# Merging the scores of two local head pairs into one six-bank step

## The chip, the cores and the metric

The kernel runs on one core of a Trainium2 chip. Its engines are TensorE (PE, with its weight loads PEld), VectorE (DVE), ScalarE (ACT), GpSimd (POOL) and SyncE (SP). Each works through its own queue in the order written; semaphores make one wait for another. The metric is device time in microseconds. PE writes its results to PSUM, which has eight banks of 128 partitions x 512 fp32 values; a bank may be filled again once the engine that reads it is through.

## The reference

Eight batches of eight heads, 576 positions, head dimension 64. Heads 0 to 3 attend locally (a key at most 31 positions back), heads 4 to 7 in a stride (keys at the same position modulo 32). The attention output, as 4608 tokens x 512, goes through a feed-forward layer with a squared Relu.

```
scores = q @ k.T / sqrt(64)
local:   0 <= i - j < 32            (heads 0..3)
strided: j <= i and i % 32 == j % 32 (heads 4..7)
attn = softmax(where(mask, scores, -1e9)) @ v
x = attn.transpose(0, 2, 1, 3).reshape(4608, 512)
out = relu(x @ w_in) ** 2 @ w_out        # w_in 512 x 2048, w_out 2048 x 512
```

## The kernel before

**The feed-forward layer is the backbone.** Tokens go in nine chunks of 512. `mm1(c, ff)` makes 128 of the 2048 hidden rows of chunk c with four matmuls of 128 x 512 (L663; one for each of the four tiles `xt[0..3]`, in the order 0, 1, 2, 3), a Relu on ACT into `r` (L669, four buffers) and a square on DVE into `g` (L670). `mm2(c, i)` adds four of the sixteen hidden blocks to 128 output rows (L685); after the fourth part ACT copies the sum to `y` (L689) and SP stores it. Each call is one *group*. Chunk c has groups 32c to 32c+15 (`mm1`) and 32c+16 to 32c+31 (`mm2`). From group 32 on all of them take turns on the two banks called `ph`.

**The attention is woven in by a written plan.** `PLAN` is a list of lines `group: words`. Before a group is issued, the words of its line are run, and each word is a step that issues its instructions on the engines at once; the group comes behind them. After each group `tick()` issues the work that was put off with `later(n, ...)`, n ticks ahead, by due time. So the plan fixes the order in every queue. Batch 0 has a list of its own ahead of group 0. A unit is a pair of heads: unit 4b and 4b+1 are the local pairs of batch b, and 4b+2 and 4b+3 the strided ones.

The words that matter here:

- `S u`: scores of a local pair (L494). One head sits on partitions 0 to 63 and the other on 64 to 127, so matmuls come in pairs that contract over 64 rows each. Six blocks of 96 queries x 128 keys for each head, 12 matmuls in four `pt` banks of 288 columns; then four exps (L504) into the tile `es[u % 4]` and two multiplications by the mask on DVE (L510). With `!` all four exps are issued at once; without, they are spread over the ticks.
- `D u.part`: output of one head of a local pair (L623, six matmuls with 128 columns of `e` as weights, so the last reads 32 columns past the head), then a reciprocal and a multiplication on DVE (L628, L629) into `x`. Before it starts it issues what is still put off for u.
- `E u`: transposes `x` into `xt[0]` or `xt[1]`: by DMA from SP for batches from 2 on (L638), by PE and a copy for batch 1.
- `s b.part` and `x b.part`: scores and products of the strided heads, in three parts. `x` uses two `pt` banks: the sums of weights (L550; Ln and Exp on ACT, L555 and L556, make their inverse) and the products (L553); DVE multiplies them into `xt[2]` and `xt[3]` (L563, L569). `x b.2` writes 64 rows of `xt[3]` for all 576 tokens of batch b.
- `T`, `W`, `k`, `B`, `c`: transposes by PE, copies and casts. `X`, `Y`: DMA transposes on SP. `Q`, `C`, `U`, `V`, `l`, `r`, `o`: loads on POOL. `m..v`: memsets of two block tiles of batch 2 on DVE (L813).

PSUM has five `pt` banks that `bank("pt")` hands out in turn, two `ph` and one `py`. In chunk 0 an `mm2` sum holds one of the `pt` banks, so four are left in turn from group 19 to 31. `py` isn't used after group 31.

Of the kernel before, what the change touches and what calls it, by code (L numbers as in the profile page):

```python
# [9 lines left out]
BF16 = mybir.dt.bfloat16  # L10
AF = mybir.ActivationFunctionType
ALU = mybir.AluOpType
# [8 lines left out]
"""  # L21
PLAN = """
0: l1q4+5 l1k4+5 z
1: r1q U1 mv1g
3: o0 mk0v
4: r1k V1
5: o1 l2k8+9 mbg mv0v
6: o2 o3 V2
8: c4qv
9: c5qv  # L30
# [4 lines left out]
14: S4  # L35
15: W1q1v
16: B10v W1k0a
17: S5! W1k1a
18: k10v mrg C2q C2k
19: k11v D4.0  # L40
20: s1.0 D4.1 B11v
21: s1.1 D5.0 U2
22: l3k12+13 s1.2
23: D5.1 x1.0
24: E4a
25: x1.1
26: E5a X2k l3q12+13
27: x1.2
28: V3
29: c9kv  # L50
# [5 lines left out]
38: T8qv C3k  # L56
39: k20v
40: U3
41: S8! k21v
42: T9qa  # L60
44: S9! D8.0
46: D8.1
47: E8
48: D9.0 Q16k s2.0
49: s2.1
50: Q17q Q16q s2.2 c12kv
51: D9.1 c12qa
52: Q17k c13kv c13qa
54: x2.0 X3q
55: E9 X3k C4k C4q  # L70
56: x2.1
57: T12ka
58: V4 T13qv T12qa
59: T13ka
60: x2.2 B30v
61: B31v
63: U4 S12!
64: X4q
65: D12.0
66: Y17 k30v  # L80
67: Y16 D12.1 S13! X4k C5q k31v
68: C5k
71: s3.0 E12 Q20k Q21q Q20q
72: Q21k s3.1
73: D13.0 D13.1
# [4 lines left out]
83: x3.1  # L90
89: x3.2
90: k40v
91: S16! k41v
95: U5 D16.0 D16.1
96: S17
97: Y20
99: X5k
100: C6k
101: X5q
102: Q25q V5 E16  # L100
# [9 lines left out]
114: k51v  # L110
116: x4.0
119: x4.1
124: V6
125: x4.2
128: U6 S20!
130: S21
133: D20.0
134: Y24 D20.1 X6k
135: E20 X6q s5.0 C7q Q28k
# [8 lines left out]
150: x5.1 k60v  # L128
152: k61v
153: x5.2  # L130
155: S24!
156: V7
157: U7
161: S25
162: D24.0
165: s6.0 D24.1
166: s6.1
# [9 lines left out]
186: x6.2  # L147
188: k70v
189: k71v
191: S28!  # L150
192: S29
197: s7.0
198: D28.0 s7.1
199: D29.0
# [10 lines left out]
def kernel(  # L165
# [9 lines left out]
    nc = tc.nc  # L175
    B, H, S, D = q.shape
# [4 lines left out]
    scale = 1.0 / (D ** 0.5)  # L181
    QL = 96
    NL = S // QL
# [12 lines left out]
    singles = ctx.enter_context(tc.tile_pool(name="singles", bufs=1))  # L196
# [13 lines left out]
    banks = {nm: [psum.tile([128, 512], FP32, name=f"{nm}{i}") for i in range(n)]  # L210
             for nm, n in (("ph", 2), ("py", 1), ("pt", 5))}
# [4 lines left out]
    def bank(nm):  # L216
        if in_b0[0] and nm == "pt":
            nm = "b0"
        t = banks[nm].pop(0)
        banks[nm].append(t)  # L220
        while id(t) in unread:
            run_due(lambda x: x[1] == unread[id(t)])
        return t
# [8 lines left out]
    mask_all = singles.tile([128, NL, QL], BF16)  # L232
# [7 lines left out]
    mask_bd = singles.tile([128, 1, W3], BF16)  # L240
    str_rows_t = {nm: singles.tile([SR, RW], BF16, name=f"{nm}_t") for nm in "qk"}
    kTl = [singles.tile([128, 32 + S], BF16, name=f"kTl{i}") for i in range(NV)]
    es = [singles.tile([128, 1280], BF16, name=f"e{i}") for i in range(4)]
    xt = [singles.tile([128, T], BF16, name=f"xt{p}") for p in range(4)]
    w_in_b = singles.tile([128, 4, d_ff], BF16)
    w_out_b = singles.tile([128, 16, d_model], BF16)
# [14 lines left out]
    st = {}  # L261
# [173 lines left out]
    def later(n, fn, key=None):  # L435
        pending.append((clock[0] + n, key, fn))

    def run_due(test):
        due = [x for x in pending if test(x)]
        for x in due:  # L440
            pending.remove(x)
        for x in sorted(due, key=lambda x: x[0]):
            x[2]()
# [23 lines left out]
    def step_S(u, mode=0):  # L467
# [39 lines left out]
        def masks(row):  # L507
            x = e[0:kn, S * row:S * (row + 1)].rearrange("p (t c) -> p t c", c=w)
            m = mask_all if local else mask_str.to_broadcast([kn, n, w])
            nc.vector.tensor_tensor(x, x, m, op=ALU.mult)  # L510
# [15 lines left out]
        later(3, lambda: expo(1, 1), u)  # L526
        later(4, lambda: masks(1), u)

    def blocks(part):
        return range(NJ * part, min(NJ * (part + 1), NB))  # L530

# [81 lines left out]
                rv.rearrange("c (j p) -> c p j", p=SP_), op=ALU.mult)  # L613

    def step_D(u, part):
        run_due(lambda x: x[1] == u)
        s = st[u]
        e = s["e"]
        rhs = s["v"].rearrange("p h t d -> p (h t) d")
        po = bank("pt")[:, 0:NL * (D + 1)].rearrange("p (n d) -> p n d", d=D + 1)  # L620
        for n in range(NL):
            c = QL * (NL * part + n)
            nc.tensor.matmul(po[:, n, :], e[:, c:c + 128], rhs[:, NL * part + n, 0:D + 1], start=True, stop=True)  # L623
        if part == 0:
            s["x"] = xl_pool.tile([QL, 2 * NL, D], BF16, name="x_l")
        x = s["x"].rearrange("p (t h) d -> p h t d", h=2)[:, part]
        rinv = small.tile([128, NL, 1], FP32, name="rinv")
        nc.vector.reciprocal(rinv[0:QL], po[0:QL, :, D:D + 1])  # L628
        nc.vector.tensor_tensor(x, po[0:QL, :, 0:D], rinv[0:QL].to_broadcast([QL, NL, D]), op=ALU.mult)  # L629
# [66 lines left out]
    A, V, G = nc.scalar.copy, nc.vector.tensor_copy, nc.gpsimd.tensor_copy  # L696
# [32 lines left out]
    def run_step(word):  # L729
        op, arg = word[0], word[1:]  # L730
        if op == "w":
            warm(int(arg))
        elif op == "c":
            cast_qk_local(int(arg[:-2]), arg[-2], ENG[arg[-1]])
        elif op == "T":
            step_T(int(arg[:-2]), arg[-2], ENG[arg[-1]])
        elif op == "W":
            step_TS(int(arg[0]), arg[1], int(arg[2]), ENG[arg[3]])
        elif op == "S":
            step_S(int(arg.rstrip("!")), int("!" in arg))  # L740
        elif op == "N":
            step_N(int(arg))
        elif op == "O":
            step_O(int(arg))
        elif op in "sx":
            (step_SS if op == "s" else step_XX)(*(int(x) for x in arg.split(".")))
        elif op == "k":
            step_K(int(arg[0]), int(arg[1]), ENG[arg[2]])
        elif op == "m":
            memset_later(arg[:-1], nc.gpsimd if arg[-1] == "g" else nc.vector)  # L750
        elif op == "D":
            u, part = arg.split(".")
            step_D(int(u), int(part))
        elif op == "E":
            step_E(int(arg.rstrip("av")), ENG.get(arg[-1]))
        elif op == "P":
            first_part([int(x) for x in arg])
        elif op == "H":
            shift_v_local(int(arg[:-1]), ENG[arg[-1]])
        elif op == "C":  # L760
            load_str_tall(int(arg[:-1]), arg[-1])
        elif op == "Q":
            load_qk_rows(int(arg[:-1]), arg[-1])
        elif op == "X":
            transpose_str(int(arg[:-1]), arg[-1])
        elif op == "Y":
            transpose_local(int(arg))
        elif op == "V":
            load_v_local_all(int(arg))
        elif op == "U":  # L770
            load_v_str(int(arg))
        elif op == "B":
            spread_v_str(int(arg[0]), int(arg[1]), ENG[arg[2]])
        elif op == "l":
            load_qk_local_sw(int(arg[0]), [int(x) for x in arg[2:].split("+")], arg[1])
        elif op == "r":
            load_str_rows(int(arg[0]), arg[1])
        elif op == "i":
            load_w_in(int(arg))
        elif op == "o":  # L780
            load_w_out(int(arg))
        elif op == "z":
            late_constants()
        else:
            raise ValueError(word)
# [100 lines left out]
    for line in PLAN.strip().splitlines():  # L886
        n, words = line.split(":")
        plan.setdefault(int(n), []).extend(words.split())
    for n, g in enumerate(groups):
        for word in plan.get(n, ()):  # L890
            run_step(word)
        g()
        tick()
# [32 lines left out]
```

## Time and profile before

| | us |
|---|---|
| median of 3 runs (303.82 to 304.15) | 303.82 |
| the profiled execution | 303.86 |
| its span | 302.2 |
| PE busy in it | 295.2 (98%) |
| DVE busy | 178.8 (59%) |
| ACT busy | 174.5 (58%) |
| POOL busy | 72.3 (24%) |
| granted TensorE clock | 1.00 |

The span runs from the first to the last instruction; 1.7 us lie around it. Groups of instructions go by their line in the kernel: L663 and L685 are the feed-forward matmuls (131.8 and 121.1 us of PE's busy time), L494 the local scores, L504 their exps, L510 their masks, L550 and L553 the strided products. An arrow in brackets behind a row names what ended the idle time before it. Matmuls are pipelined: one of 512 columns is shown 379 ns long though the next starts earlier, so their rate is read from starts.

### The profile page before, as it was taken

The page shows a single profiled execution, that of the slowest core. Times are in us where ns is not written, and L with a number is a line of the kernel's source. Part 1 is how long each engine was busy: PE and PEld are TensorE (multiplying, and loading weights), DVE is VectorE, ACT ScalarE, POOL GpSimd, SP SyncE. Part 2 cuts the span into 40 slices and gives each one's busy share as a digit, 9 for nine tenths or more (in the row PEclk, how much of TensorE's full clock was granted, in tenths as well). Part 3 has the DMA queues.
Part 4 walks back from the last instruction along what each step waited for, and adds up shares of the span by engine and source line. Part 5 has one row for each costly group of instructions (what it writes and reads, how often), then busy time and mean ns, then how long its engine had stood idle before and what let it go on. Part 6 is the DMA issues. An engine that isn't in the chain of part 4 may idle for free.

```text
span 302.2 us, 5752 instructions
## 1 busy us (share of the span) xinstructions
PE 295.2 (98%) x2181; PEld 146.2 (48%) x2181; DVE 178.8 (59%) x463; ACT 174.5 (58%) x344; POOL 72.3 (24%) x105
## 2 busy tenths in 40 slices
PE   8989999999999999999999999999999999999996
PEld 3543555445545544444445445444454444444444
DVE  5668688688578686585568485666486524104400
ACT  3677855777667743874387447744875346226611
POOL 8835734008104027082300840000000000000000
PEclk9999999999999999999999999999999999999999
DMA  8999999997999999999999999611110110010011
GB/s 157 181 208 200 191 199 193 166 196 117 145 171 159 159 175 190 151 138 123 177 143 151 118 198 177 123 48 68 45 23 20 73 69 0 35 72 35 0 71 70
DMA packets 93643, 37.28 MB, mean 123 GB/s; under 512 B 78956, under 2 KB 87750, under 8 KB 93616
## 3 DMA queue, kind: packets, MB, share of 16 engines
q0 software_dynamic: 54960, 18.82, 62.4%
q1 hardware_dynamic: 38512, 18.03, 31.9%
q8 instruction: 17, 0.28, 0.4%
q14 instruction: 10, 0.08, 0.1%
q10 hardware_dynamic: 144, 0.07, 0.1%
HBM read 38.21 MB, written 9.44 MB: 158 GB/s over the span
## 4 chain that ended last, share of the span: by engine, by line
PE 89%; DVE 4%; POOL 3%; ACT 2%; issue 1%; DVEq 0%; ACTq 0%; POOLq 0%
PE ph L663 39%; PE ph L685 36%; PE pt L494 2%; PE pt L623 2%; DVE xt L563 2%; PE pt L454 1%; PE pt L539 1%; PE pt L553 1%; PE ph L710 1%; PE py L685 1%; PE pt L550 1%; POOL w_in_b L426 1%; DVE g_sb L670 1%; PE pt L685 1%; ACT r L669 1%
## 5 line engine op out<-in xcount | busy, mean ns | idle before, releaser
L663 PE MATMUL ph<-xt,w_in_b 128*128 128x512 bf16 x568 | 131.8, 379 | 0.8 <-ACT xt L648 0.8
L685 PE MATMUL ph<-w_out_b,g_sb 128*128 128x512 bf16 x528 | 121.1, 379 | 0.1
L669 ACT ACTIVATE r<-ph 128x512 bf16<-128x512 f32 x142 | 84.7, 599 | 34.9 <-PE ph L663 30.0
L670 DVE TENSOR_TENSOR g_sb<-r 128x512 bf16<-128x512 bf16 x144 | 60.2, 423 | 65.6 <-ACT r L669 64.9
L663 PEld LDWEIGHTS <-w_in_b 128*128 128x128 bf16 x576 | 53.0, 97 | 59.3 <-issue 1.9
L685 PEld LDWEIGHTS <-g_sb 128*128 128x128 bf16 x560 | 51.7, 97 | 57.2 <-DVE g_sb L670 0.5
L689 ACT COPY y<-ph 128x512 f32<-128x512 f32 x33 | 19.5, 590 | 53.5 <-PE ph L685 53.5
L563 DVE TENSOR_TENSOR xt<-pt,rv 64x144 bf16<-64x144 f32 x84 | 34.0, 405 | 18.0 <-ACT rv L556 16.8
L504 ACT ACTIVATE e<-pt 128x288 bf16<-128x288 f32 (+1 forms) x68 | 24.0, 414 | 7.8 <-PE pt L494 7.7
L629 DVE TENSOR_TENSOR x_l<-pt,rinv 96x384 bf16<-96x384 f32 x30 | 16.6, 554 | 1.0
L555 ACT ACTIVATE rv<-pt 128x432 f32<-128x432 f32 (+1 forms) x21 | 10.5, 501 | 11.1 <-PE pt L550 11.1
L569 DVE TENSOR_TENSOR xt<-pt,rv 64x270 bf16<-64x270 f32 (+1 forms) x28 | 10.9, 432 | 8.5 <-ACT rv L556 8.3
L510 DVE TENSOR_TENSOR e<-e,mask_all 128x576 bf16<-128x576 bf16 x28 | 12.4, 453 | 4.1 <-ACT e L504 3.8
L540 ACT ACTIVATE e<-pt 128x432 bf16<-128x432 f32 (+1 forms) x21 | 10.4, 497 | 6.0 <-PE pt L539 6.0
L351 POOL DMA_DIRECT2D q_t<-in_q_dram x6 | 3.5, 579 | 43.4 <-DMA qT_s<-q_t 43.4
L420 POOL DMA_DIRECT2D vl<-in_v_dram x7 | 10.0, 1435 | 12.7 <-DMA vl<-in_v_dram 10.5
L280 POOL DMA_DIRECT2D k_l<-in_k_dram x16 | 12.1, 761 | 2.8 <-DMA v_st<-in_v_dram 1.7
L280 POOL DMA_DIRECT2D q_l<-in_q_dram x16 | 11.6, 730 | 3.5 <-DMA k_l<-in_k_dram 1.9
L623 PEld LDWEIGHTS <-e 128*128 128x128 bf16 x192 | 9.0, 97 | 5.3 <-issue 0.4
L556 ACT ACTIVATE rv<-rv 128x432 f32<-128x432 f32 (+1 forms) x21 | 11.2, 532 | 0.7
L623 PE MATMUL pt<-vl,e 128*128 128x65 bf16 x180 | 9.9, 193 | 0.0
L351 POOL DMA_DIRECT2D k_t<-in_k_dram x6 | 3.2, 540 | 27.0 <-DMA kT_s<-k_t 27.0
(129 smaller groups left out, 219.7 us busy)
## 6 DMA issues: line engine op xcount, KB each, us to landing
out_dram<-y SPq DMA_DIRECT2D x35, 256.0 KB, 3.7
vl<-in_v_dram POOLq DMA_DIRECT2D x7, 384.0 KB, 12.5
w_in_b<-in_moe_w_in_dram POOLq DMA_DIRECT2D x4, 512.0 KB, 12.3
w_out_b<-in_moe_w_out_dram POOLq DMA_DIRECT2D x4, 512.0 KB, 13.5
q_t<-in_q_dram POOLq DMA_DIRECT2D x7, 288.0 KB, 6.2
k_t<-in_k_dram POOLq DMA_DIRECT2D x7, 288.0 KB, 5.6
v_st<-in_v_dram POOLq DMA_DIRECT2D x7, 216.0 KB, 8.0
k_l<-in_k_dram POOLq DMA_DIRECT2D x16, 72.0 KB, 7.5
```

The lines of the kernel that those rows point to most:

```text
L280: nc.gpsimd.dma_start(out=t[:, :, hh, :], in_=src[b, 2 * p + hh].rearrange("(t p) d -> p t d", p=QL))
L504: nc.scalar.activation(e[0:kn, lo:lo + S // 2], pss[row][half][0:kn, 0:S // 2], AF.Exp, scale=scale)
L510: nc.vector.tensor_tensor(x, x, m, op=ALU.mult)
L556: nc.scalar.activation(rv, rv, AF.Exp, scale=-1.0)
L563: nc.vector.tensor_tensor(to[:, :, NJ * part:NJ * (part + 1), par], of, by, op=ALU.mult)
L623: nc.tensor.matmul(po[:, n, :], e[:, c:c + 128], rhs[:, NL * part + n, 0:D + 1], start=True, stop=True)
L629: nc.vector.tensor_tensor(x, po[0:QL, :, 0:D], rinv[0:QL].to_broadcast([QL, NL, D]), op=ALU.mult)
L663: nc.tensor.matmul(ph, w_in_b[:, kk, 128 * ff:128 * (ff + 1)], xt[kk][:, 512 * c:512 * (c + 1)], start=(kk == order[0]), stop=(kk == order ...
L669: nc.scalar.activation(r, ph, AF.Relu)
L670: later(1, lambda: nc.vector.tensor_tensor(g[:, ff, :], r, r, op=ALU.mult))
L685: nc.tensor.matmul(py, g[:, ff, 128 * j:128 * (j + 1)], w_out_b[:, ff, :], start=(ff == 0), stop=(ff == 15))
L689: nc.scalar.copy(y, py)
```

## The change

Three things change.

- A new word `G b` replaces the two `S` words of batch b, for b from 2 to 7. It computes the scores of both local pairs in one go: 24 matmuls into six `pt` banks of 384 columns (three for each row half), then six exps of 384 columns, issued at once, first those of row half 0; the masks of half 0 come two ticks later and those of half 1 three. The results of both pairs lie in one tile `es01` of 2560 columns, of which `es[0]` and `es[1]` are now slices. `D` reads from the new place for units above 7.
- From group 32 on `py` joins the `pt` banks, which makes six.
- The plan moves words. `G` stands before groups 47, 63, 94, 124, 158 and 191. In batch 2 the steps `D8`, `D9`, `E8`, `E9`, `s2` and `x2` move; `D12`, `D16` and `x4.2` move as well. In batch 1 `S5` moves behind `W1k1a`, and `E5a` ahead of `x1.1`; two DVE memsets move to group 1.

The diff, with plan lines that only lose or shift words around these left out where "..." stands:

```diff
-1: r1q U1 mv1g
-3: o0 mk0v
+1: r1q U1 mv1g mk0v mv0v
+3: o0
 4: r1k V1
-5: o1 l2k8+9 mbg mv0v
+5: o1 l2k8+9 mbg
...
-17: S5! W1k1a
-18: k10v mrg C2q C2k
+17: W1k1a
+18: S5! k10v mrg C2q C2k
...
-25: x1.1
-26: E5a X2k l3q12+13
+25: E5a x1.1
+26: X2k l3q12+13
...
-41: S8! k21v
+41: k21v
 42: T9qa
-44: S9! D8.0
-46: D8.1
-47: E8
-48: D9.0 Q16k s2.0
-49: s2.1
-50: Q17q Q16q s2.2 c12kv
-51: D9.1 c12qa
-52: Q17k c13kv c13qa
-54: x2.0 X3q
-55: E9 X3k C4k C4q
-56: x2.1
-57: T12ka
+47: G2
+48: Q16k
+50: Q17q Q16q c12kv s2.0
+51: c12qa D8.0 s2.1
+52: Q17k c13kv c13qa D8.1
+53: D9.0 E8 s2.2
+54: X3q D9.1
+55: X3k C4k C4q x2.0
+56: E9
+57: T12ka x2.1
...
-63: U4 S12!
+63: G3 U4
 64: X4q
-65: D12.0
 66: Y17 k30v
-67: Y16 D12.1 S13! X4k C5q k31v
-68: C5k
+67: Y16 X4k C5q k31v D12.0
+68: C5k D12.1
...
-91: S16! k41v
-95: U5 D16.0 D16.1
-96: S17
+91: k41v
+94: G4
+95: U5
 97: Y20
-99: X5k
+98: D16.0
+99: X5k D16.1
...
-124: V6
-125: x4.2
-128: U6 S20!
-130: S21
+124: G5 V6
+128: U6 x4.2
...
-155: S24!
...
-161: S25
+158: G6
...
-191: S28!
-192: S29
+191: G7
...
-    es = [singles.tile([128, 1280], BF16, name=f"e{i}") for i in range(4)]
+    es01 = singles.tile([128, 2560], BF16, name="e01")
+    es = [es01[:, 0:1280], es01[:, 1280:2560]] + [singles.tile([128, 1280], BF16, name=f"e{i}") for i in (2, 3)]
...
+    def step_G(b):
+
+        us = (4 * b, 4 * b + 1)
+        bk = [bank("pt") for _ in range(6)]
+        bk = [bk[0::2], bk[1::2]]
+        for t in range(2 * NL):
+            for row in range(2):
+                s, j = st[us[t // NL]], t % NL
+                rows, c = slice(64 * row, 64 * row + 64), QL * (t % 4)
+                nc.tensor.matmul(bk[row][t // 4][:, c:c + QL], s["kT"][rows, QL * j:QL * j + 128],
+                                 s["qT"][rows, QL * j:QL * (j + 1)], start=True, stop=True)
+        e = es01[:, 0:4 * S].rearrange("p (r c) -> p r c", r=2)
+
+        def masks(row):
+            x = e[:, row].rearrange("p (u t c) -> p u t c", u=2, c=QL)
+            for i in range(2):
+                nc.vector.tensor_tensor(x[:, i], x[:, i], mask_all, op=ALU.mult)
+
+        for row in range(2):
+            for i in range(3):
+                nc.scalar.activation(e[:, row, 4 * QL * i:4 * QL * (i + 1)], bk[row][i][:, 0:4 * QL], AF.Exp, scale=scale)
+            later(row + 2, lambda row=row: masks(row), ("G", b, row))
...
-        run_due(lambda x: x[1] == u)
+        run_due(lambda x: x[1] in (u, ("G", u // 4, part)))
         s = st[u]
-        e = s["e"]
+        e = es01[:, 2 * S * part + S * (u % 4):] if u > 7 else es[u % 4][:, S * part:]
...
-            c = QL * (NL * part + n)
+            c = QL * n
...
+        elif op == "G":
+            step_G(int(arg))
...
+        if n == 32:
+            banks["pt"] += banks.pop("py")
```

## The prediction

> **What bounds the kernel now.** I read the page first, then the waits, then the timeline of single engines around the places that the change touches.
>
> ```profile
> span 302.2 us, 5752 instructions
> ...
> PE 295.2 (98%) x2181; PEld 146.2 (48%) x2181; DVE 178.8 (59%) x463; ACT 174.5 (58%) x344; POOL 72.3 (24%) x105
> ```
>
> TensorE (PE) is busy for 98% of the span, so the end is set by its queue: time comes from matmul time taken away, and goes to whatever makes PE wait. ACT and DVE have 40% free on average, but both take their work strictly in the order written, so one burst can hold PE up. Who waits:
>
> ```profile
> ACT r L669 <- DVE g_sb L670: 3.0, 6, 0.7
> ...
> PE pt L494 <- ACT e L504: 0.5, 1, 0.5
> ...
> PE pt L645 <- DVE xt L563: 0.3, 1, 0.3
> ```
>
> The first line says that a Relu cannot start before VectorE has squared an older `r` (four buffers); the other two are batch 1's second scores waiting for an exp, and a transpose waiting for a bank that the strided multiplies still read. Now a score step in mid-run (S12 before group 63), PE alone, then ACT alone; columns are start, length, what:
>
> ```profile
> 85.22 2.75 PE L685 MATMUL ph<-w_out_b,g_sb 128*128 128x512 bf16 x12
> 87.90 0.43 PE L494 MATMUL pt<-qT,kTl 64*128 64x96 bf16 x12
> 88.26 1.04 PE L685 MATMUL ph<-w_out_b,g_sb 128*128 128x512 bf16 x4
> 89.14 1.03 PE L663 MATMUL ph<-xt,w_in_b 128*128 128x512 bf16 x4
> 90.00 0.35 PE L623 MATMUL pt<-vl,e 128*128 128x65 bf16 x6
> 90.19 1.89 PE L663 MATMUL ph<-xt,w_in_b 128*128 128x512 bf16 x8
> ```
>
> ```profile
> 85.12 0.59 ACT L689 COPY y<-ph 128x512 f32<-128x512 f32 x1 [0.23 <-PE ph L685]
> 85.60 0.45 ACT L555 ACTIVATE rv<-pt 128x324 f32<-128x324 f32 x1
> 86.08 0.47 ACT L556 ACTIVATE rv<-rv 128x324 f32<-128x324 f32 x1
> 88.24 1.32 ACT L504 ACTIVATE e<-pt 128x288 bf16<-128x288 f32 x4 [1.69 <-PE pt L494]
> 89.42 0.62 ACT L689 COPY y<-ph 128x512 f32<-128x512 f32 x1
> ```
>
> A big matmul comes every (2.75 - 0.38)/11 = 0.216 us, a group of four takes 0.864. From 85.22 to 88.26 are 3.04 us; twelve big matmuls are 2.59, so the twelve score matmuls cost 0.45. They run as six pairs (two 64-row halves); the last pair starts at 88.33 - 0.20 = 88.13, so a pair takes (88.13 - 87.90)/5 = 0.045, six of them 0.27, and going in and out of these 64-row matmuls about 0.19.
>
> The copy of y (group 63) had its last matmul near 88.92 + 0.38 and started at 89.42, just behind four exps. Group 65 takes the bank that it reads: copy done at 90.04, group 65 at 90.19. The slack is 0.15, with D12.0 (0.18) in between.
>
> **The change part by part.** The sum is against the profiled execution: 303.86 us with a span of 302.2; the median of the runs is 303.82.
>
> *Scores merged, six batches.* G has 24 score matmuls as before, but goes in and out once: 0.19 + 12 x 0.045 against 2 x 0.45, a saving of 0.2 a batch, **-1.2**. Waits that went with the old steps: eight big matmuls take 1.73 us when undisturbed; after S8 they took 1.82 and after S13 1.91 (chain and PE timeline), because Relus stood behind exps: 0.10 + 0.17, **-0.28**.
>
> *ACT under G.* Four exps of 288 columns start (1.32 - 0.42)/3 = 0.30 apart, and the copy followed 1.18 after the first: 0.295 each. For 384 columns I scale to 0.393; six are 2.36, against 8 x 0.295 = 2.36 for two S. ACT's work is unchanged, but it comes in one block. [...]
>
> Let T0 be where PE would have begun the next big matmul. S12 began at T0 + 0.09 and its first exp three pairs and 0.34 later; G's first banks need four pairs: first exp at T0 + 0.47, ACT free at T0 + 2.83.
>
> *G3 before 63 and G7 before 191.* The group runs from T0 + 0.71; its y copy is behind six exps: T0 + 2.83 to 3.43, PE sees it 0.06 later at 3.49. The second group after wants that bank at 0.71 + 2 x 0.864 = 2.44. **+1.05** for G7. D12.0, which hid this before, has moved to 67. Bounds 0.9 (0.37 an exp) to 1.1.
>
> At 63 something else lands too. SP issues transposes in order; before, E9 (x of unit 9) stood ahead of X3k, at 79.80, and X3k at 82.34 held the queue for 3.52. E9 now comes behind X3k and a y store, and E8, moved from 47 to 53, directly ahead of X3q. The issue-to-landing times in that stretch are 8.7 (E9), 10.6 (X3q), 7.4 (X3k), so E9 landed at 88.5, 0.9 before group 64 reads it (89.14 + 0.216). Behind X3k it lands about 1.5 to 2.5 later in the same frame; a miss of 0.6 to 2. It overlaps with the bank's wait, so I take the larger of the two, **+1.3** (1.0 to 2.2).
>
> *G4 (94), G6 (158).* The y copy of 95 or 159 is ready at T0 + 2.64, starts at 2.83, is done by 3.49; group 97 or 161 wants the bank at 3.30. Something under 0.2 each; Relus have slack behind. **+0.15** (0 to 0.4).
>
> *G2 before 47.* Group 46's Relu comes first, so exps begin at T0 + 0.69 and group 47's Relu at 3.05, done at 3.65. On DVE its square (0.34 to the next) stands ahead of the masks, which then run from 4.03 to 4.87 (0.46 each, 0.38 apart). PE reaches D8.0 at 0.71 + 4 x 0.864 + 0.20 (s2.0) = 4.37; its last matmul, 0.15 later, reads into the second mask's columns and sees them at 4.93. **+0.4** (0 to 0.6).
>
> *G5 (124) and x4.2, moved from 125 to 128.* This is the largest term. PE and what follows, before:
>
> ```profile
> 147.84 0.30 PE L550 MATMUL pt<-e,ones_bd 128*128 128x324 bf16 x1
> 147.98 0.32 PE L553 MATMUL pt<-e,vb 128*128 128x54 bf16 x6
> 148.14 2.75 PE L685 MATMUL ph<-w_out_b,g_sb 128*128 128x512 bf16 x12
> 150.82 0.43 PE L494 MATMUL pt<-qT,kTl 64*128 64x96 bf16 x12
> 151.18 1.04 PE L663 MATMUL ph<-xt,w_in_b 128*128 128x512 bf16 x4
> ```
>
> x4.2 at 147.84 makes Ln (148.18), Exp (148.65) and four multiplies into `xt[3]` (149.15 to 150.72): 2.88 us. Chunk 4 (groups 128 to 143) covers tokens 2048 to 2559, and batch 4 begins at 2304, so the fourth matmul of group 128 reads what x4.2 writes. Before, three groups and a score step covered this. Now x4.2 stands directly ahead of 128: position P, products until P + 0.30, fourth matmul wanted at P + 0.95. The copy of y of group 127 is ahead of the Ln on ACT (ready at P + 0.2, the Ln 0.48 after it, as at 85.12 and 85.60), which delays it by 0.34. Multiplies done at P + 2.88 + 0.34 = 3.22, seen at 3.28: **+2.34** (2.0 without the copy, 2.5). PE is in order, nothing passes.
>
> *Front: two memsets to group 1.* They ran at 25.59 (before group 3) and 27.67 (before 5), 1.23 each; now both precede the square of group 3, which goes from 26.74 to about 28.0 to 28.2. The Relu of group 7 waits for it (r buffers), so it starts at 28.4 to 28.7 instead of 27.20, and group 9, which needs its bank, at 29.0 to 29.3 instead of 27.85. Against that T4qa no longer waits for its cast (0.68 before, PE held until 30.25) nor T4kv (0.12). Net 0.35 to 0.67; memsets came after idles of 0.24 and 0.34, so I take **+0.6**; without those idles it is the lower end.
>
> *Batch 1's second scores, 17 to 18.* Group 16 began at 37.03 and group 17 at 39.27: 2.24, of which group 16 is 0.86, S5 0.45 and eight transposes 0.26. The other 0.66 is S5, whose last matmuls waited until 38.77 for the exp of 38.27; with W1k1a ahead, and a group later, the bank is free in time. But E5a and x1.1 share group 25, and its product bank is x1.0's (four banks rotate while a y holds one): x1.0's six multiplies start 46.65 in the new frame and end 49.16, x1.1 wants the bank at 47.94. +1.28, against E5a's old wait of 0.45. -0.66 - 0.45 + 1.28 = **+0.2** (-0.2 to 0.4).
>
> Other moves (x2.0 and x2.1 a group later, D8 and D9 to 51 to 54, U6 and V6 on POOL's queue) issue the same work; I cost them at nothing, since POOL waits 43 us for X transposes anyway and x2.2's bank is now T12ka's, which is read early.
>
> Sum: -1.2 - 0.28 + 1.05 + 1.3 + 0.15 + 0.4 + 2.34 + 0.6 + 0.2 = +4.56, so **308.4**.
>
> **The rivals.**
>
> *x4.2 hidden.* Should the dependence be looser than I read, or P later because ACT and DVE are early, the 2.34 go and 306.1 stays. For it: only 64 rows of `xt[3]` are written. Against: the program must be right, and the columns overlap. 0.1.
>
> *Transposes worse.* The hardware queue ran at landing times of 7 to 11 us there. If E8 and E9 land 3 to 5 late, 310.3 to 312. Against: software loads pause from 79.8 to 90.3 on POOL, and landing later in the run is 3.6. 0.1.
>
> *The other side: the order written is not the order run.* If the queues were filled in another order (copies ahead of exps, x4.2's products ahead of group 125, memsets behind squares), the added waits, 5.84 in all, go and -1.48 + 0.2 remains, 302.6; it decides once no more than 1.3 of the 5.84 is left. Against: at 88.24 the four exps ran in one piece ahead of the copy, and PE's rows follow the plan word by word. 0.07.
>
> **How the numbers follow.** My forecast as summed has 0.72 (306.4 with all low ends, 310.3 with all high), x4.2 hidden 0.1 (305.2 to 306.6), transposes 0.1, the other side 0.07, and 0.01 is unnamed. The range 305.4 to 310.3 leaves out the other side and most of the transposes. About 0.2%, 0.6 us, can be told from no change: faster 0.04, same 0.03, slower 0.93.
>
> **What would show it.** A wait of PE at a L663 matmul on DVE's `xt` of about 2.3 near group 128 and one on ACT's y of about 1 after G7; an ACT group of six 128x384 exps near 2.4; PE on DMA or ACT at group 64; an ACT wait on `g_sb` of over 1 near 28; scores at 0.73 for 24 matmuls. If group 128 starts without that wait, the prediction falls by its largest term.

## The result and the profile after

The changed kernel takes 308.63 us in the median of four executions (308.06 to 309.89), the kernel before beside it 303.82: a ratio of 1.0153, 95% interval [1.0129, 1.0176], so it is slower by 1.5%. The profiled execution is the one of 308.06, with a span of 306.4 against 302.2. The forecast was 308.4 and slower. (Where a kernel below had executions more than 1.5% above its fastest, as the first mended try did, its median and ratio leave these out.)

From the page of the changed kernel, first the span, then TensorE's share, the clock that TensorE was granted in forty slices, and the group of the merged exps (busy us, mean ns | idle before them):

```profile
span 306.4 us, 5689 instructions
...
PE 291.1 (95%) x2144; PEld 146.2 (48%) x2181; DVE 178.8 (58%) x463; ACT 174.1 (57%) x332; POOL 71.3 (23%) x105
...
PEclk9999999999999999999999999999999999999999
...
L544 ACT ACTIVATE e<-pt 128x384 bf16<-128x384 f32 x30 | 12.8, 510 | 6.8 <-PE pt L533 6.8
```

TensorE went from 98% busy to 95%; the other engines do what they did. (Part of PE's fall is only that the trace lacks 37 matmul records: 2144 are listed, 2181 weight loads. A later trace of the same kernel that has them all shows 96%, and there 1.7 us of it are matmuls at half clock.) What PE waits for, in us in total, times, longest:

```profile
PE ph L681 <- DVE xt L587: 2.2, 1, 2.2
PE ph L681 <- ACT y L707: 1.6, 2, 0.8
PE ph L681 <- ACT r L687: 1.4, 1, 1.4
...
PE pt L571 <- DVE xt L581: 1.1, 1, 1.1
```

None of these four lines has a counterpart before. They are, in order: the fourth matmul of group 128 waiting for x4.2's multiplies; groups 65 and 193 waiting for a copy of y; group 9 waiting for a Relu; x1.1 waiting for its bank. Together 6.3 us of new waits, against a span only 4.2 us longer.

The largest one, PE alone, then ACT, then DVE (start, length):

```profile
152.61 0.30 PE L568 MATMUL pt<-e,ones_bd 128*128 128x324 bf16 x1
152.75 0.32 PE L571 MATMUL pt<-e,vb 128*128 128x54 bf16 x6
152.91 0.81 PE L681 MATMUL ph<-xt,w_in_b 128*128 128x512 bf16 x3
155.88 1.45 PE L681 MATMUL ph<-xt,w_in_b 128*128 128x512 bf16 x6 [2.16 <-DVE xt L587]
```

```profile
152.81 0.59 ACT L707 COPY y<-ph 128x512 f32<-128x512 f32 x1 [1.28 <-PE ph L703]
153.29 0.45 ACT L573 ACTIVATE rv<-pt 128x324 f32<-128x324 f32 x1
153.77 0.47 ACT L574 ACTIVATE rv<-rv 128x324 f32<-128x324 f32 x1
```

```profile
154.27 1.55 DVE L587 TENSOR_TENSOR xt<-pt,rv 64x270 bf16<-64x270 f32 x4 [2.25 <-ACT rv L574]
```

Three matmuls of group 128 run, the fourth starts at 155.88, when the four multiplies (end 155.82) are through. Undisturbed it would have come at 152.91 + 3 x 0.216 = 153.56: 2.32 lost. The y copy stands ahead of the Ln, as the forecast had it.

The block of exps and its victim, at G7, PE and then ACT:

```profile
217.00 1.03 PE L681 MATMUL ph<-xt,w_in_b 128*128 128x512 bf16 x4
218.82 1.02 PE L681 MATMUL ph<-xt,w_in_b 128*128 128x512 bf16 x4 [0.80 <-ACT y L707]
```

```profile
215.89 0.87 ACT L544 ACTIVATE e<-pt 128x384 bf16<-128x384 f32 x2 [2.28 <-PE pt L533]
216.65 0.50 ACT L544 ACTIVATE e<-py 128x384 bf16<-128x384 f32 x1
217.02 1.27 ACT L544 ACTIVATE e<-pt 128x384 bf16<-128x384 f32 x3
218.13 0.64 ACT L707 COPY y<-ph 128x512 f32<-128x512 f32 x1
```

Six exps from 215.89 to 218.13, then the copy to 218.77, then group 193 at 218.82. Undisturbed it would have started at 217.00 + 0.864, so 0.96 are lost. Group 65 after G3 loses the same 0.96.

And the front, DVE and ACT:

```profile
26.96 1.23 DVE L833 MEMSET vb<- 128x1408 f32 x1 [0.24 <-issue]
28.11 1.02 DVE L688 TENSOR_TENSOR g_sb<-r 128x512 bf16<-128x512 bf16 x3
```

```profile
28.56 1.09 ACT L687 ACTIVATE r<-ph 128x512 bf16<-128x512 f32 x2 [1.82 <-DVE g_sb L688]
```

The squares start at 28.11, behind both memsets; the Relu of group 7 stands still for 1.82 until the first is done, and group 9 comes at 29.21, 1.54 late. A little later S4 stands longer, too (PE):

```profile
34.91 0.75 PE L489 MATMUL pt<-qT,kTl 64*128 64x96 bf16 x12
```

Before, the same twelve took 0.48. The eighth comes at 35.38, behind VectorE's copy of W1q0v's transposes out of PSUM (34.88 to 35.33), whose bank it needs; before, that copy ended at 34.50 and the eighth came at 34.55.

### The profile page after: what moved, and what is told of

Its sections match the earlier page's. It is cut to its first block, busy times and chain, and to the rows that moved or that the text cites. A ratio compares the mean times of both kernels' runs of the same rounds, so it can differ in the third digit from the quotient of the medians.

```text
span 306.4 us, 5689 instructions
## 1 busy us (share of the span) xinstructions
PE 291.1 (95%) x2144; PEld 146.2 (48%) x2181; DVE 178.8 (58%) x463; ACT 174.1 (57%) x332; POOL 71.3 (23%) x105
## 4 chain that ended last, share of the span: by engine, by line
PE 86%; ACT 5%; DVE 4%; issue 2%; DMA 2%; POOL 0%; DVEq 0%; ACTq 0%; POOLq 0%
PE ph L681 37%; PE ph L703 35%; DMA w_out_b<-in_k_dram 2%; DVE xt L581 2%; PE pt L641 1%; ACT e L544 1%; PE pt L557 1%; PE ph L728 1%; PE py L703 1%; PE pt L571 1%; PE pt L533 1%; PE pt L568 1%; ACT r L687 1%; PE pt L703 1%; PE pt L449 1%
## 5 line engine op out<-in xcount | busy, mean ns | idle before, releaser
L703 PE MATMUL ph<-w_out_b,g_sb 128*128 128x512 bf16 x511 | 118.4, 379 | 1.3 <-issue 0.6
L581 DVE TENSOR_TENSOR xt<-pt,rv 64x144 bf16<-64x144 f32 x72 | 29.1, 404 | 14.9 <-ACT rv L574 14.0
L544 ACT ACTIVATE e<-pt 128x384 bf16<-128x384 f32 x30 | 12.8, 510 | 6.8 <-PE pt L533 6.8
L540 DVE TENSOR_TENSOR e<-e,mask_all 128x576 bf16<-128x576 bf16 x24 | 9.9, 456 | 8.7 <-ACT e L544 8.7
L573 ACT ACTIVATE rv<-pt 128x432 f32<-128x432 f32 (+1 forms) x18 | 9.0, 502 | 9.9 <-PE pt L568 9.9
L647 DVE TENSOR_TENSOR x_l<-pt,rinv 96x384 bf16<-96x384 f32 x24 | 13.3, 553 | 0.8
L587 DVE TENSOR_TENSOR xt<-pt,rv 64x270 bf16<-64x270 f32 (+1 forms) x24 | 9.3, 429 | 7.0 <-ACT rv L574 6.9
L571 PEld LDWEIGHTS <-vb 128*128 128x128 bf16 x154 | 7.1, 97 | 4.8 <-issue 1.3
```

What stands on the lines that cost most here:

```text
L544: nc.scalar.activation(e[:, row, 4 * QL * i:4 * QL * (i + 1)], bk[row][i][:, 0:4 * QL], AF.Exp, scale=scale)
L571: nc.tensor.matmul(po[:, c], vb[:, t, :], e[:, c], start=True, stop=True)
L581: nc.vector.tensor_tensor(to[:, :, NJ * part:NJ * (part + 1), par], of, by, op=ALU.mult)
L703: nc.tensor.matmul(py, g[:, ff, 128 * j:128 * (j + 1)], w_out_b[:, ff, :], start=(ff == 0), stop=(ff == 15))
```

## The experiments

Twelve kernels ran. Each was compared with the kernel before on the same chip; its ratio comes from that. For the size of single terms I also give the lowest time, to be set against the changed kernel's lowest, 308.06. The runs come from three chips; the kernel before has nearly the same lowest time on each of them (303.75, 303.66, 303.67). The waits given as "extra" are read from the starts of the big matmuls: spacing, less 0.216 for each, less the small matmuls between them.

### x4.2 ahead of group 121

```
 119: x4.1
+121: x4.2
 124: G5 V6
-128: U6 x4.2
+128: U6
```

> The changed kernel with x4.2 before group 121 and nothing else moved. My theory (group 128 reads what x4.2 writes into xt[3], and three groups used to cover its 2.9 us): the wait of 2.3 us at group 128's fourth matmul goes, the profiled span falls from 306.4 to about 304.1, the median from 308.6 to about 306.3. Rival (the wait is one for a bank that G5 holds, or for the DMA of E17, and x4.2 was only the last to be seen): the wait stays at group 128 or appears at x4.2 or G5, at least 1.8 us of it, and the time moves by less than 0.5.

Measured 306.15 (305.93 to 307.93), ratio 1.0064 [1.0043, 1.0084], span 304.2. Group 128 runs through without a gap. From lowest to lowest it is -2.13, against the 2.32 of the wait. The rest is a new wait of 0.22 in the scores of G5: x4.2's four multiplies now run from 147.76 to 149.32, and G5's last seven matmuls start at 149.38. The largest term of the forecast stands, and its rival (the dependence looser than read) falls. About half of the loss against before comes from the place of one word in the plan.

### x4.2 one group earlier

```
+127: x4.2
-128: U6 x4.2
+128: U6
```

> x4.2 is issued one group earlier, at 127 in place of 128. Theory that the wait at group 128 is the fixed chain of 3.2 us behind x4.2: one group of 0.86 covers part of it, wait at the fourth matmul 2.33 - 0.86 = 1.47 us (1.1 to 1.5, since the copy of y of group 127 now comes behind the Ln), 307.2 us at clock 1.0. On the clock: the front's wait of 1.54 us never went with a fall of the granted clock, the one of 2.2 to 2.3 did in half of the executions. If the length of the pause decides, no execution has clock .994 (all near 307.2); if any pause of over 1 us at this place does it, about half are near 308.8 with clock .994.

Measured 306.96 (306.83 to 307.05), ratio 1.0103 [1.0089, 1.0117]. ACT, and then PE:

```profile
152.77 0.47 ACT L575 ACTIVATE rv<-rv 128x324 f32<-128x324 f32 x1
153.32 0.59 ACT L708 COPY y<-ph 128x512 f32<-128x512 f32 x1
```

```profile
154.89 1.46 PE L682 MATMUL ph<-xt,w_in_b 128*128 128x512 bf16 x6 [0.96 <-DVE xt L588]
```

The extra is 1.12, at the low end: one group covers 0.86, and the copy of y now comes behind the Ln and the Exp, which frees the other 0.34 that the forecast had put on it (2.33 - 0.86 - 0.34 = 1.13). So the chain behind x4.2 is the forecast's, link by link. All four executions had the full clock, which the section on the clock below needs.

### The two memsets back to groups 3 and 5

```
-1: r1q U1 mv1g mk0v mv0v
-3: o0
+1: r1q U1 mv1g
+3: o0 mk0v
-5: o1 l2k8+9 mbg
+5: o1 l2k8+9 mbg mv0v
```

> The changed kernel with the two DVE memsets again before groups 3 and 5. My theory (the pair in one piece delays the square of group 3, so the Relu of group 7 has no r buffer and group 9 no bank): the wait of 1.5 us at group 9 goes, but the one of 0.7 at the first transpose of batch 1's q and 0.1 at the next come back; net -0.66 us. Rival (PE waits there for what arrives by DMA, whatever the memsets do): the waits at group 9 keep over 1 us, net within 0.2.

Measured 307.5 (307.06 to 308.92), ratio 1.0109 [1.0081, 1.0137]. Group 9's wait is gone, S4 takes what it took before, and the old waits at T4qa (0.61) and T4kv (0.30) are back: -1.54 - 0.27 + 0.61 + 0.30 = -0.9. Lowest to lowest -1.0.

### A fifth buffer for the Relus

```
-    r_pool = ctx.enter_context(tc.tile_pool(name="r_pool", bufs=4))
+    r_pool = ctx.enter_context(tc.tile_pool(name="r_pool", bufs=5))
```

> The changed kernel with five r buffers in place of four, memsets where the change put them. My theory (the Relu of group 7 waits for the square of group 3 behind the memsets): now it is group 8's Relu that waits for that square, so PE stops at group 10 and not at 9, about 0.6 in place of 1.5, and up to 0.3 of it shows at the first transpose behind its cast; net -0.6 to -0.9 us. Rival (PE waits for the loads or for the casts behind the memsets): the whole 1.5 us stays, in that place or at the transpose.

Measured 308.89 (307.6 to 309.26), ratio 1.0127 [1.0088, 1.0166]. The wait moves on by one group, to group 10, and shrinks from 1.54 to 0.67; T4qa and T4kv wait again for 0.14 and 0.11, S4 by 0.24 less than in the changed kernel. Net -0.86 in the trace, within the -0.6 to -0.9 expected; lowest to lowest it is only -0.46, from three executions at full clock, so the time shows less than the trace. The move and the shrinking of the wait are what the theory asks for: it was the buffers of `r` through which the memsets reached TensorE.

### The last three exps spread over the ticks

```
-        for row in range(2):
-            for i in range(3):
-                nc.scalar.activation(...)
-            later(row + 2, lambda row=row: masks(row), ("G", b, row))
+        def expo(row, i):
+            nc.scalar.activation(...)
+        for i in range(3):
+            expo(0, i)
+            later(i + 1, lambda i=i: expo(1, i), ("G", b, 1))
+        later(2, lambda: masks(0), ("G", b, 0))
+        later(4, lambda: masks(1), ("G", b, 1))
```

> The changed kernel with the last three exps of each G put off by one, two and three ticks, so that copies and Relus come between. My theory (the six exps in one block keep the copy of y, and so a ph bank): the waits of 0.96 at groups 65 and 193, of 0.1 at 97 and 161 and of 0.3 at D8.0 go, together -2.4 us. Rival 1 (group 64 or 65 has to wait for the transposed x of E9 anyway): -1.5, with a wait on a DMA at 64. Rival 2 (a Relu that shares its group with an exp takes over 0.86 us, so Relus fall behind one after another): of the 2.4 some 1 to 2 come back as waits of 0.1 to 0.3 at the groups behind G3 and G7.

Measured 307.79 (306.17 to 308.93), ratio 1.0112 [1.0083, 1.0141]; lowest to lowest -1.89. PE and ACT at G7:

```profile
216.02 3.19 PE L685 MATMUL ph<-xt,w_in_b 128*128 128x512 bf16 x14
```

```profile
215.66 0.50 ACT L543 ACTIVATE e<-py 128x384 bf16<-128x384 f32 x1
216.22 0.59 ACT L711 COPY y<-ph 128x512 f32<-128x512 f32 x1
216.70 0.50 ACT L543 ACTIVATE e<-pt 128x384 bf16<-128x384 f32 x1
217.08 0.60 ACT L691 ACTIVATE r<-ph 128x512 bf16<-128x512 f32 x1
```

The copy of y slips in behind the third exp and group 192 runs on into 193 without a gap. The waits at 65, 97, 161, 193 and D8.0 are all gone (0.96 + 0.10 + 0.10 + 0.96 + 0.32 = 2.44); a new one of 0.46 stands at D12.1, whose mask now comes last, so the trace gives -1.98 where -2.4 was expected. ACT has the same exps to do: only the order of its queue cost the time.

### E5a behind x1.1

```
-25: E5a x1.1
-26: X2k l3q12+13
+25: x1.1
+26: E5a X2k l3q12+13
```

> The changed kernel with E5a again a group behind x1.1 (words 25 and 26 as before). My theory (x1.1's product bank is x1.0's as long as E5a comes ahead of it): x1.1 takes an older bank, its wait of 1.24 goes and E5a waits about 0.45 as it did before the change; net -0.8 us. Rival (x1.0's six multiplies on DVE set the pace, so that PE loses the same wherever it waits for them): the waits sum to 1.1 to 1.3 in the new place, net within 0.2.

Measured 308.31 (307.19 to 309.24), ratio 1.0122 [1.0092, 1.0152]. x1.1's extra of 1.24 is gone, and E5a has one of 0.66: -0.58, lowest to lowest -0.87. That is the exchange that the forecast priced; E5a's wait came back larger than the 0.45 that it had before the change.

### TensorE kept busy through the pause

Nine matmuls of 512 columns into a free bank, ahead of group 128; nothing reads their result.

```
+        if n == 128:
+            pw = bank("pt")
+            for _ in range(9):
+                nc.tensor.matmul(pw, w_in_b[:, 0, 0:128], w_in_b[:, 0, 0:512], start=True, stop=True)
```

> The changed kernel with nine matmuls of 512 columns, whose result nobody reads, into a free bank between x4.2 and group 128. They fit inside PE's wait there (9 x 0.216 = 1.94 of 2.33 us). My theory (a wait of over 2 us at that place sometimes lets TensorE's granted clock fall to a half for some 3.4 us afterwards, 1.6 to 1.7 us lost, which parts the runs of the variants with this wait into two bunches): no run shows the clock at 0.994, all lie in the lower bunch, 308.0 to 308.7, and the wait left is 0.4 or less with the same total. Rival (the clock falls for a reason of its own, temperature or another wait): a third to a half of the runs still lie 1.6 higher at 0.994.

Measured 308.17 (308.07 to 309.19), ratio 1.0116 [1.0076, 1.0156], granted clock 0.999 or 1.0 in all six executions. The extra left at group 128 is 0.41, and the lowest time is the changed kernel's (308.07 for 308.06), as it should be when the added matmuls only fill a wait. Two of the six, 308.82 and 309.19, lie above the 308.7 expected. What led to it, and what follows for the clock, is told below. The execution of 309.19 was profiled, and had a wait that the first trace of the changed kernel did not have:

```profile
PE ph L681 <- DMA xt<-x_l: 1.7, 1, 1.7
```

### The changed kernel once more

> The changed kernel once more, unedited, to see its own spread beside the others on one chip. If the pause of 2.3 us before group 128's fourth matmul lowers the clock as often as in the four variants that keep it (12 of 24 executions), about half of these are at .994 and near 309.7; if the four executions seen at first were typical, all are at clock 1.0, between 308.0 and 309.9.

Measured 309.68 (308.55 to 310.38), ratio 1.019 [1.017, 1.0209]; three of four executions at clock 0.994 (309.64, 309.72, 310.38), one at 1.0 (308.55). So neither count that I had set out was typical. The profiled execution is the longest, 310.38, and shows both of the things that made it so. First group 64, PE and then SP's queue:

```profile
90.37 0.38 PE L681 MATMUL ph<-xt,w_in_b 128*128 128x512 bf16 x1
92.22 1.46 PE L681 MATMUL ph<-xt,w_in_b 128*128 128x512 bf16 x6 [1.47 <-DMA xt<-x_l]
```

```profile
79.89 3.09 SPq L351 DMA_TRANSPOSE qT_s<-q_t  x1
83.06 2.81 SPq L351 DMA_TRANSPOSE kT_s<-k_t  x1
...
86.60 2.25 SPq L656 DMA_TRANSPOSE xt<-x_l  x1
```

The second matmul of group 64 waits for E9, which was issued at 86.60 behind X3q and X3k and landed 5.6 us later. It is 1.63 late (92.22 - 90.37 - 0.216). The copy of y for group 65 is done meanwhile, so this takes the place of the 0.96, as the forecast had it: the larger of the two counts. In the execution of 308.06 E9 was issued at 86.13 and landed in 2.8 us, at 88.9, in time. It is not E9 alone that is slower here: E8, X3q and X3k ahead of it took 7.2, 9.5 and 7.1 us to land, against 5.7, 6.9 and 5.5 in the execution of 308.06.

Then the clock, in windows of one us (PE, PEld, DVE, ACT, POOL, then the granted clock, DMA, GB/s):

```profile
155.00:156.00 1.00, 0.00 (x0) 0.00 (x0) 0.99 (x3) 0.00 (x0) 0.00 (x0) 1.00 0.69 244
156.00:157.00 1.00, 0.47 (x2) 0.25 (x2) 0.47 (x2) 0.01 (x1) 0.00 (x0) 0.86 0.86 142
157.00:158.00 1.00, 1.00 (x3) 0.30 (x2) 0.39 (x1) 0.58 (x1) 0.00 (x0) 0.50 0.52 93
158.00:159.00 1.00, 1.00 (x4) 0.43 (x3) 0.04 (x1) 0.31 (x1) 0.00 (x0) 0.50 0.48 98
159.00:160.00 1.00, 1.00 (x4) 0.33 (x3) 0.42 (x1) 0.29 (x1) 0.00 (x0) 0.50 1.11 179
160.00:161.00 1.00, 1.00 (x5) 0.39 (x4) 0.02 (x1) 0.60 (x1) 0.00 (x0) 0.93 0.81 122
```

As the wait for x4.2 ends, TensorE comes back at half its clock. Eight big matmuls then take 0.427 instead of 0.216: 1.69 us. With 1.69 and the 0.67 by which E9 exceeds the copy of y, 308.06 becomes 310.42; measured were 310.38.

### E9 ahead of X3k

```
-55: X3k C4k C4q x2.0
-56: E9
+55: E9 X3k C4k C4q x2.0
```

> Only the place of E9 (the transpose of x of unit 9) on SP's queue is changed: it stands between X3q and X3k again, as in the kernel before. Theory that E9 behind X3k lands late in some executions of the changed kernel and makes its spread at full clock (308.06 to 309.89): no wait of TensorE on a DMA near group 64, E9 lands before 87.5 us, executions at clock 1.0 all between 307.6 and 308.5. Rival, that E9's place is without effect and the spread has another origin: executions at clock 1.0 reach 309 and above again. Executions at clock .994 may be near 309.7 in either case, since the wait at group 128 stays.

Measured 308.2 (308.06 to 310.0), ratio 1.0157 [1.0136, 1.0177]; one execution at clock 0.994 (310.0), the four others 308.06 to 308.49. The number fits the theory, the mechanism doesn't. SP's queue:

```profile
83.74 1.46 SPq L655 DMA_TRANSPOSE xt<-x_l  x1
85.30 4.65 SPq L350 DMA_TRANSPOSE kT_s<-k_t  x1
```

E9 is issued 2.4 earlier than in the changed kernel's profile, but takes 7.1 to land, at 90.84, and not before 87.5; group 64 wants it at 90.52 + 0.22 = 90.74 and is held for about 0.1. So changing places with X3k moves the landing less than the landing itself varies (2.8 to 7.1 us in these traces). That E9's place makes the spread is therefore not shown; that E9 is late in some executions is (here, in the run above, and with TensorE kept busy).

### The kernel before with the front mended

The memsets go to GpSimd at 27, S5 behind W1k1a, x1.1 and x1.2 a group later each.

```
-3: o0 mk0v
+3: o0
-5: o1 l2k8+9 mbg mv0v
+5: o1 l2k8+9 mbg
-17: S5! W1k1a
-18: k10v mrg C2q C2k
+17: W1k1a
+18: S5! k10v mrg C2q C2k
-25: x1.1
-26: E5a X2k l3q12+13
-27: x1.2
-28: V3
+25: E5a
+26: X2k l3q12+13 x1.1
+27: mk0g mv0g
+28: x1.2 V3
```

> The kernel before with its two-step scores, and only the front mended: both memsets on POOL at group 27, S5 behind W1k1a at 18, E5a at 25, x1.1 at 26, x1.2 at 28. My theory: the waits for the casts (0.69 + 0.12) and for S5's exp (0.66) go, x1.1 waits about 0.4 as E5a did: -1.4, some 302.5 us. Rival (POOL's memsets delay its loads, or x1.2 comes too late for group 32): 0.5 to 1 of it comes back as a wait at 32 or on a DMA.

Measured 303.41 (302.75 to 307.26), ratio 0.9987 [0.9955, 1.002]: no difference that can be told. The front's waits and S5's went, but in the profiled execution (304.62) others came: the first chunk starts 0.45 later, behind a wait of 1.3 for a load in batch 0, S8 waits 0.47 for VectorE's copy of qT, and about 1.0 is lost at S9 and D8.0, of it 0.4 on a load of v. The loads are issued by GpSimd, and the memsets now stand among them; that these are the cause was not tried apart.

### The changed kernel with its waits taken away, first try

The front as above, G2 at 48, G4 at 93, G6 at 157, G7 at 189 with its last three exps spread, x4.2 at 121, D12.1 at 69.

```
-25: E5a x1.1
-26: X2k l3q12+13
-27: x1.2
-28: V3
+25: E5a
+26: X2k l3q12+13 x1.1
+27: mk0g mv0g
+28: x1.2 V3
...
-47: G2
-48: Q16k
+48: G2 Q16k
...
-94: G4
+93: G4
...
+121: x4.2
...
-158: G6
+157: G6
...
-191: G7
+189: k71v G7
```

> The same front as in before_mended, with the six-bank scores of the change: G2 at 48, G4 at 93, G6 at 157, G7 at 189, x4.2 at 121, D12.1 at 69, and G3 alone with its last three exps each a tick later. My theory: none of the waits that the change brought is left, and what the merged scores are worth by themselves shows: six times 0.2, and the waits of 0.10 and 0.17 behind S8 and S13; 1.5 us below before_mended, some 301.0. Rival (the merged scores gain nothing once they are placed where nothing waits, since the score matmuls are as many): within 0.3 of before_mended.

Measured 306.42 in seven of twelve executions (302.9 to 307.41; the other five took 308.23 to 312.65, at clocks of 0.988 to 0.994), ratio 1.0025 [0.9981, 1.007]: no difference that can be told. The waits that it was to remove are gone, and in most executions the gain with them. The one wait that leads the list of the profiled execution, PE around it, and the window behind it:

```profile
PE ph L689 <- DMA xt<-x_l: 3.1, 1, 3.1
```

```profile
87.70 0.38 PE L689 MATMUL ph<-xt,w_in_b 128*128 128x512 bf16 x1
91.16 2.38 PE L689 MATMUL ph<-xt,w_in_b 128*128 128x512 bf16 x7 [3.08 <-DMA xt<-x_l]
```

```profile
92.00:93.00 1.00, 1.00 (x4) 0.40 (x3) 0.37 (x1) 0.98 (x2) 1.00 (x3) 0.50 0.96 176
```

TensorE reaches group 64 2.7 earlier than in the changed kernel, E9 does not come earlier (issued at 84.68, landed 6.4 later), and behind the pause of 3.1 the clock is at half again. The wait (91.16 - 87.70 - 0.216 = 3.24) and half of the 3.4 us at half clock make an estimated 4.9 us: without them this execution would have taken about 301.5. So most of the gain was given back at one transpose, which the first trace of the changed kernel had not listed as a wait. The longer executions were not traced.

### The same with E9 ahead of both strided transposes

```
-27: mk0g mv0g
-29: c9kv
+29: mk0g mv0g c9kv
...
-54: X3q D9.1
-55: X3k C4k C4q x2.0
-56: E9
+54: D9.1
+55: E9 X3q X3k C4k C4q x2.0
...
-157: G6
+158: G6
```

> All the changed kernel's waits taken away as in the mended version tried before (x4.2 at 121, memsets on GpSimd, now at group 29 where it waits anyway, the x1 products spread, G2 at 48, G4 at 93, G7 at 189 with its last exps spread, the second row of values at 69), and E9 now ahead of both X3 transposes on SP, G6 at 158 as in the changed kernel. Theory that E9 on SP's queue was what ate the mended version's gain: no wait on a DMA at group 64, no clock under .99, 301.5 us (300.9 to 302.5), 0.8% below the kernel before. Rival, that SP's transposes as a whole are late once TensorE runs earlier (X3q and X3k come 2 to 3 us later): a wait on the strided projections or the x products of batch 3 in groups 57 to 75, 303 to 305. Second rival, that merging is worth nothing beyond its waits: 303 to 304 with no wait left.

Measured **301.71** (301.49 to 302.66), ratio 0.9943 [0.993, 0.9957]: faster than the kernel before, and all executions at clock 0.999 or 1.0. The page's span and TensorE's share, and the two largest waits of PE:

```profile
span 299.8 us, 5727 instructions
...
PE 293.5 (98%) x2181; PEld 146.3 (49%) x2181; DVE 178.8 (60%) x461; ACT 174.5 (58%) x332; POOL 73.6 (25%) x107
```

```profile
PE py L744 <- DVE xt L846: 1.3, 1, 1.3
PE ph L687 <- ACT xt L672: 0.8, 1, 0.8
```

Both were there before the change. E9 now leaves SP at 77.4, right behind E8 and 7 us earlier than in the first try, and with 7.6 to 8.2 us to landing both are there in time, 85.6 at the latest against 88 for group 64. X3q and X3k leave 2 later than in the first try, and no wait comes of it: the first rival falls. Two other lines differ from the first try (the memsets, G6), so that the gain is E9's alone is not shown; that the wait at group 64 went is. The span is 2.4 shorter than before, and the starts of the matmuls account for it: merged scores -1.2, the waits after S8 and S13 -0.27, S5 -0.66, E5a -0.45, T4qa and T4kv -0.81; left over are S4 +0.27, x1.1 +0.37, G5 +0.24 (x4.2's multiplies, as at 121 above) and a first chunk that starts 0.12 later: -2.4. About 1.3 of that is the front (S5, E5a, T4qa and T4kv, less S4 and x1.1), and 1.2 the merging (scores and the two waits, less G5). The times agree: from the lowest of the kernel before with its front mended to the lowest here it is -1.26.

## Why the prediction was right

The time (308.63 for 308.4) and the sign came out, and so did the mechanism of the largest terms: the chain behind x4.2, and copies that stand behind a block of exps. How close the sum came is partly luck. The memsets cost 0.4 more than forecast and G3 0.34 less, which nearly cancels. And the first row agrees by a rounding: the prediction's own 0.19 + 12 x 0.045 = 0.73 against 0.90 saves 0.17 a batch, 1.0 in all; it took 0.2, and what was measured, 0.713 against 2 x 0.457, happens to give 0.2. Extras in the profiled executions, after less before:

| term | forecast | profile | shown by |
|---|---|---|---|
| merged scores, six batches | -1.2 | -1.2 (24 matmuls take 0.713) | starts of the big matmuls |
| waits after S8, S13 | -0.28 | -0.27 | the same |
| G7, copy of y behind six exps | +1.05 | +0.96 | exps spread |
| G3, the same or E9 | +1.3 | +0.96; 1.63 where E9 is late | exps spread; the kernel once more |
| G4, G6 | +0.15 | +0.19 | exps spread |
| G2 and D8.0 | +0.4 | +0.32 | exps spread |
| x4.2 ahead of 128 | +2.34 | +2.32 | x4.2 at 121 and at 127 |
| memsets at the front | +0.6 | +1.0 (1.54 + 0.27 - 0.69 - 0.12) | memsets back; fifth buffer |
| S5, E5a, x1.1 | +0.2 | +0.13 (1.24 - 0.66 - 0.45) | E5a behind x1.1 |
| sum | +4.56 | +4.4 | span: +4.2, with a first chunk that starts 0.11 earlier |

- The two y copies were put a little too high because of the exps. Scaled from 288 to 384 columns by their length, I took 0.393 each; six run in 2.24, or 0.373 each. The step that failed is the scaling: 0.295 for 288 and 0.373 for 384 make, by an estimate from these two alone, 0.81 ns for each further column and a fixed part of 0.06, which a scaling by length multiplies too.
- The front was put too low. Group 9 came at 29.21, within the 29.0 to 29.3 of the forecast, and the old waits of T4qa and T4kv went as it said; the step that failed is to end there and to count the old waits as gained in full. S4 takes 0.27 more, which no step named, and the term lies above its own bounds of 0.35 to 0.67. The memsets are not the cause of this 0.27: it stands as well in the traces of the kernel before with its front mended and of the second mended try, where the two memsets run on GpSimd. In all of them T4qa and T4kv no longer wait, and VectorE's copy of W1q0v's transposes comes behind another copy and a square (33.85 to 34.88 in the changed kernel), so part of the time that the old waits took is now spent at S4.
- In the profiled execution the term at G3 was 0.96 and not 1.3, since E9 landed in 2.8 us; with the landings of 5.6 in two other traces (the kernel once more, TensorE kept busy) it is 1.63 and 1.86. The first lies just under the forecast's 1.0 to 2.2, the others within it. I had priced one landing where there is a spread.
- The rivals: x4.2 was not hidden; the order written was the order run, at each of the places shown above; the transposes got worse, by 0.7 where the changed kernel's trace shows it, against the 1.9 to 3.6 of that rival (the execution of 309.89, at full clock and 1.8 above the lowest, was not traced and may be such a case). The first mended try shows what they cost once TensorE runs earlier.
- What no step had: the clock. All steps took TensorE's matmul at 0.216, and where the 2.3 us pause halves the clock that is off by 1.7 us. It doesn't show in the profile of 308.06, but three of the eight executions of the changed kernel had it, and one of those (310.38) ended above the range's 310.3. So here, too, the agreement of 308.4 with the first median is closer than the terms deserve: without a fall of the clock and a late E9 the time is 308.06, with the one or the other 308.7 to 309.7.

## What the runs showed of the hardware that was not expected

**A pause of 2.3 us can halve TensorE's clock for 3.4 us.** A mean clock of 0.994 over the run is one such stretch: (1 - 0.5) x 3.4 / 307 = 0.0055. Counting executions by the pause at group 128:

| pause | kernels | executions | at clock 0.994 |
|---|---|---|---|
| 2.3 us | the changed one (twice), memsets back, exps spread, E5a behind x1.1, fifth buffer, E9 ahead of X3k | 37 | 16 |
| 1.1 us | x4.2 at 127 | 4 | 0 |
| 0.4 us | TensorE kept busy | 6 | 0 |
| none | x4.2 at 121 | 9 | 1 |
| none | second mended try | 5 | 0 |

In four of the seven traces of the first row the fall comes at the end of that pause (0.05 us before it to 0.75 after it), and with TensorE kept busy at this place the clock stays, though nothing else moves: its windows from 152 to 161 us all have 1.00. So without the pause these falls did not come (0 of 6 executions against 16 of 37).

Why 16 of 37 and not all is not shown. The table sets PE's longest pause in nine traces against the fall, whose edges are worked out from the mean clock of windows of one us and good to about 0.02:

| trace | PE idle, us | the pause ends at | clock behind it at 0.50 from | to |
|---|---|---|---|---|
| first mended try (wait for E9) | 3.08 | 91.16 | 91.98 | past 95.00 |
| E5a behind x1.1 | 2.2 | 155.21 | 155.92 | 159.34 |
| fifth buffer | 2.2 | 155.03 | 155.78 | 159.20 |
| the changed kernel once more | 2.2 | 156.53 | 156.72 | 160.14 |
| memsets back | 2.17 | 155.07 | 155.02 | 158.44 |
| TensorE kept busy (wait for E9) | 1.69 | 92.70 | none | |
| exps spread | 2.2 | 155.00 | none | |
| E9 ahead of X3k | 2.2 | 156.00 | none | |
| the changed kernel, first trace | 2.16 | 155.88 | none | |

The four whole falls last 3.42 each, and the clock in them is 0.50. Pauses of 2.2 stand on both sides, so their length alone doesn't decide, and no run tried what else does. Behind the 3.08 the clock fell, behind the 1.69 it did not. Big matmuls start 0.427 apart at half clock, as they also do at the start of the run (from 1.67 to 3.38 us in the changed kernel's first trace, four steps).

The wait of 1.5 us at the front had no fall behind it in any trace here. Some executions of the kernel before have 0.994 as well (3 of 51, at 306.6 to 307.8 us), and one of x4.2 at 121; none of them was traced, so what lowered the clock there stays open.

**The landing of a transpose varies more than one place in the queue moves it.** E9 landed 2.8, 5.6, 6.4 and 7.1 us after its issue in four traces, and its issue took 1.2 to 2.8 us of SP's time. Behind both strided transposes it was there at 88.9 in one trace of the changed kernel and at 92.2 in the other; ahead of X3k alone at 90.8. Only ahead of both was it clearly earlier, at 85.6.

## What to carry to other kernels

A step moved by one word can cost more than a merge saves: before moving it, follow its whole chain (here products, Ln, Exp, four multiplies: 3.2 us) to the first matmul that reads the result, leave enough groups between to cover it (here four of 0.86), and see whose banks its last link holds meanwhile. Work that is merged into one block on an engine that is half idle still delays whatever stands behind it in that engine's queue (here a copy of y, and with it TensorE by 0.96); issue the first half at once and the rest between the others' work. And when waits are taken away, TensorE arrives earlier behind them (here 2.7 at group 64): look up which transfers had landed only just in time, and move their issue too, or the gain goes into them, and, as behind the waits of 2.2 and 3.1 us here, into the clock.
